# Window attention with sinks and a highway layer: K, Q and V loads issued at three points of a block, and the t bias in four pieces

## The chip, the cores and the metric

The kernel runs on one core of one Trainium2 chip. The metric is the device time of one execution in microseconds (us); the time before is the median of three runs. A second source is one execution recorded by the profiler. In it PE is the matmuls of TensorE, PEld its weight loads, DVE is VectorE, ACT is ScalarE, POOL is GpSimd, and SP issues DMAs.

## The reference

Attention with 4 sink keys and a window of 128, over 4 batches, 8 heads, 768 tokens and a head size of 64; then a highway layer on the 3072 tokens of 512 numbers.

```python
scores = q @ k.T / 8
keep = (key < 4) | ((row - key >= 0) & (row - key < 128))
a = softmax(where(keep, scores, -1e9))
x = (a @ v) as [3072, 512]
H = max(x @ w_h, 0)
T = 1 / (1 + exp(-(x @ w_t + b_t)))
out = T * H + (1 - T) * x
```

Inputs and output are 32-bit floats.

## The kernel before, in words

The tokens are cut into 24 blocks of 128, six for each batch. The key and value tiles lie half a block (64 tokens) off the query tiles, so that a query block meets its own shifted key tile in full and one half of each neighbour. For each block n the kernel does these steps, and a text called ORDER lists all steps of all blocks by hand as `step:block`. Each engine runs its own instructions in the order in which ORDER names them, so two neighbours on different engines may be exchanged there without a change in either engine's order.

- `S` (`pe_S`, L619): TensorE transposes the query and key tiles of a later block (L323; from block 8 on, S:n transposes q and k of block n+2) and makes the scores of block n (L376, L389). One query tile, that of block 9, has a transpose of its own, `Tq:9`.
- `xx` or `x0_`, `x1_`: ScalarE takes the exponential (L403, L398). `tt`, `tq`, `tk` copy the transposed tiles out of PSUM (L335, L328).
- `mm` or `m0_`, `m1_`: VectorE multiplies by the mask (L409).
- `sk`, `es`: scores and exponentials of the sink keys (L358, L365).
- `A` (`pe_A`, L445): values times weights. First `pe_AB` (L427) does the shifted halves as 16 matmuls of 64x64 (L434): their contraction rows are one half of the array's rows, their output partitions the other half. Then 8 full matmuls (L453) and 2 for the sinks (L459) follow.
- `xh` (L467, L472): VectorE normalises, the result is x in 16 bits. `X` transposes it (L486), `xT` or `xTV` copies it out.
- `Mh` (L514) and `Mt` (L502): four 512-column matmuls each with w_h and w_t. `u` is ScalarE's tanh (L507), `U` adds one (L526), `d` is max(h,0)-x (L520), `e` their product (L531), `o` the output (L536), which SP stores.

The bias b_t is added to the t product by a matmul with rows of ones. `bt16` holds half of b_t in rows 0 and 64 and zeros elsewhere. For blocks under 8, `pe_Mt` starts with one 128x128 matmul of 512 columns (L499). From block 9 on, `pe_A(n)` first calls `pe_bias(n-1)` (L439), which does the same for block n-1 with two matmuls of 64x64 and 512 columns (L442), one in rows and columns 0 to 63 of the array, one in 64 to 127. Two constant tiles serve this: `ones_row` (row 0 ones) and `ones2` (rows 0 and 64 ones), both made by VectorE in step `mc`, `bias_rows` (L262).

Loads of q, k and v are DMAs that GpSimd issues, one after the other in its queue, each turning 32 bits into 16. Those of the first nine blocks are written out ahead of ORDER (L210 to L238), except q8. The rest belong to step A:n, in this order:

```python
load_v(n + 4)      # from 9
load_q(n + 6)      # from 8
load_k(n + 6)      # from 9
```

From block 9 on q and k have three buffers each (`late_pool`), so that q12 takes the buffer of q9 and k12 that of k9; v has five slots. A load whose buffer is still in use waits in GpSimd's queue, and all behind it wait too. A load that begins a batch (k12, v12 and so on) is two DMAs of half the size. GpSimd also fills the sink keys and values of batches 1 to 3 (`fill_ks`, L347, and `sink_v`, L186) when `tk` or `tt` has copied the first key tile of the batch.

Of the kernel before, what the change touches and what calls it, by code (L numbers as in the profile page):

```python
# [20 lines left out]
def kernel(  # L21
# [18 lines left out]
    nc = tc.nc  # L40
# [46 lines left out]

    ctx.callback(close_s)
    HP = P // 2
    B0 = 9  # L90
    M0 = 9
    FIRST = 9
    NV = FIRST + 5
# [15 lines left out]
    def load_q(n):  # L109
        b, c = divmod(n, NSC)  # L110
        qsd = (sd_pool if n < FIRST else late_pool).tile([P, H, D], FP16, tag="qsd", name="qsd")
        nc.gpsimd.dma_start(out=qsd, in_=q[b, :, c * P:(c + 1) * P, :].transpose([1, 0, 2]))  # L112
        q_sd[n] = qsd

    def load_k(n):
        ksd = (sd_pool if n < FIRST else late_pool).tile([P, H, D], FP16, tag="ksd", name="ksd")
        for rows, b, s0 in chunk_parts(n):
            nr = rows.stop - rows.start
            nc.gpsimd.dma_start(out=ksd[rows], in_=k[b, :, s0:s0 + nr, :].transpose([1, 0, 2]))  # L119
        k_sd[n] = ksd  # L120
# [20 lines left out]
    bt32 = const.tile([P, DM], FP32, tag="bt32")  # L141
    bt16 = const.tile([P, DM], FP16, tag="bt16")
    ones_row = const.tile([P, P], FP16, tag="ones_row")
    ones2 = const.tile([P, P], FP16, tag="ones2")
    kf_first = const.tile([P, H, D], FP32, tag="kf0", name="kf0")
    ident32 = const.tile([P, P], FP32, tag="ident32")
    ident2 = const.tile([P, P], FP16, tag="ident2")
    ks_bd = [const.tile([P, KW], FP16, tag=f"ks{i}", name=f"ks{i}") for i in range(2)]
    vs_bd = [const.tile([P, H, 65], FP16, tag=f"vs{i}", name=f"vs{i}") for i in range(2)]
# [112 lines left out]
    def bias_rows(_):  # L262
        nc.vector.memset(bt16, 0.0)
        nc.vector.memset(ones_row, 0.0)
        nc.vector.memset(ones_row[0:1, :], 1.0)
        nc.vector.tensor_copy(out=ones2, in_=ones_row)
        nc.vector.memset(ones2[HP:HP + 1, :], 1.0)

    def bias_half(_):
        for r in (0, HP):  # L270
# [13 lines left out]
    def m_tile():  # L284
        return m_bank[int(next(m_next))]
# [141 lines left out]
    def pe_AB(n):  # L427
        av = av_tile(n)
        nxt = v_ring[vi(n + 1)]
        prv = v_ring[vi(n - 1 if n % NSC else n)]  # L430
        lo, hi = slice(0, HP), slice(HP, P)
        for j in range(H):
            for src, part, vt, h in ((lo, hi, nxt, j), (hi, lo, prv, (j + 4) % H)):
                nc.tensor.matmul(  # L434
                    av[part, h // 4, h % 4, 0:_AVN], lhsT=e_at(n, h)[src, P:EW],
                    rhs=vt[src, 65 * h:65 * h + _AVN], start=(h % 4 == 0), stop=False,
                    skip_group_check=True)

    def pe_bias(n):  # L439
        t_of[n] = m_tile()  # L440
        for rows in (slice(0, HP), slice(HP, P)):
            nc.tensor.matmul(t_of[n][rows, :], lhsT=ones2[rows, rows], rhs=bt16[rows, :],  # L442
                             start=True, stop=False, skip_group_check=True)

    def pe_A(n):  # L445
        if n >= B0:
            pe_bias(n - 1)
        pe_AB(n)
        av = av_of[n]
        vt = v_ring[vi(n)]  # L450
        b, c = divmod(n, NSC)
        for h in range(H):
            nc.tensor.matmul(  # L453
                av[:, h // 4, h % 4, 0:_AVN], lhsT=e_at(n, h)[:, 0:P],
                rhs=vt[:, 65 * h:65 * h + _AVN], start=False,
                stop=False, skip_group_check=True)
# [174 lines left out]
    def new_T(m, g):  # L631
        if g and m and m % NSC == 0 and m < NB:
            fill_ks(m // NSC, nc.gpsimd)
            sink_v(m // NSC, nc.gpsimd)

    def do_A(n):
        pe_A(n)
        if FIRST <= n + 4 <= NB:
            load_v(n + 4)
        if AHEAD <= n + 6 < NB:  # L640
            load_q(n + 6)
        if FIRST <= n + 6 <= NB:
            load_k(n + 6)

    def norm(n):
        dve_rec(n)
# [2 lines left out]
    def spare(t):  # L649
# [5 lines left out]
        "tqV": lambda n: copy_T(n, 0, nc.vector.tensor_copy),  # L655
        "tkV": lambda n: copy_T(n, 1, nc.vector.tensor_copy),
        "xx": act_SS, "tt": both_T, "mm": dve_masks,
        "S": pe_S, "x0_": lambda n: act_S(n, 0), "x1_": lambda n: act_S(n, 1),
        "m0_": lambda n: dve_mask(n, 0), "m1_": lambda n: dve_mask(n, 1),
        "sk": pe_sink, "es": act_sink, "A": do_A, "xh": norm,  # L660
        "X": pe_X, "xT": act_X, "xTV": lambda n: act_X(n, nc.vector.tensor_copy),
        "Mh": pe_Mh, "Mt": pe_Mt, "u": act_u, "U": dve_U, "d": dve_d, "e": dve_e, "o": dve_o,
# [12 lines left out]
    }  # L675
    ORDER = """
    mz0_:0 ma:0 na:0 Tq:0 na:1 Tk:0 tq:0 mz1_:0 tk:0 ma:1 wA:0 wA:0 Tk:1 mc:0 cv:0 tk:1 fa:0
    wA:0 wA:0 wA:0 S:0 cv:1 x0_:0 fb:0 x1_:0 wA:0 wA:0 wA:0 wA:0 Tq:3 m0_:0 fc:0 tq:3 wA:0 Tk:2
    tk:2 m1_:0 fd:0 wA:0 wA:0 wA:0 wA:0 Tq:1 A:0 tq:1 S:1 xh:0 sk:1 x0_:1 x1_:1 Tq:2 m0_:1 X:0
    sk:3 xTV:0 es:1 Tk:3 m1_:1 tq:2 tk:3 wA:1 A:1 es:3 S:2 xh:1 x0_:2 x1_:2 Tk:4 m0_:2 sk:2  # L680
    tkV:4 X:1 es:2 m1_:2 S:3 xT:1 A:2 x0_:3 Mh:1 x1_:3 xh:2 tq:4 d:1 X:2 tk:5 Mh:0 xTV:2 m0_:3
    Mh:2 d:0 m1_:3 S:4 d:2 Mt:0 x0_:4 x1_:4 m0_:4 A:3 u:0 m1_:4 Mt:1 tq:5 xh:3 tk:6 U:0 sk:4 u:1
    e:0 S:5 es:4 o:0 X:3 x0_:5 U:1 sk:5 xTV:3 e:1 A:4 x1_:5 m0_:5 o:1 tq:6 Mt:2 xh:4 tk:7 es:5
# [8 lines left out]
    d:11 S:14 xT:12 U:11 A:13 e:11 xx:14 o:11 Mh:12 xh:13 tt:14 Mt:12 mm:14 X:13 d:12 u:12 S:15  # L692
# [4 lines left out]
    A:18 xx:19 U:16 e:16 sk:19 xh:18 Mt:17 es:19 mm:19 tt:19 Mh:17 o:16 u:17 X:18 S:20 d:17  # L697
    xT:18 U:17 A:19 xx:20 e:17 o:17 Mh:18 xh:19 tt:20 Mt:18 mm:20 X:19 u:18 S:21 xTV:19 d:18
    A:20 xx:21 U:18 e:18 sk:21 o:18 Mt:19 es:21 xh:20 tt:21 Mh:19 mm:21 u:19 X:20 S:22 d:19
    xT:20 U:19 A:21 xx:22 e:19 o:19 Mh:20 xh:21 tk:24 Mt:20 mm:22 X:21 u:20 S:23 xTV:21 d:20  # L700
    A:22 xx:23 U:20 e:20 sk:23 xh:22 Mt:21 es:23 mm:23 X:22 u:21 Mh:21 xT:22 o:20 A:23 d:21 U:21
# [45 lines left out]
```

## Time and profile before

| What | Value |
|---|---|
| median of three runs | 120.45 us (120.37 to 120.69) |
| the profiled execution, its own time | 134.59 us |
| its span, first to last instruction | 132.5 us |
| granted TensorE clock in it, mean | 0.760 of full speed |
| GpSimd's load instruction (q, k, v) | 0.91, 0.86, 0.85 us each |
| from issue to landing, median (q, k, v) | 5.7, 5.7, 5.4 us |
| t bias before A, L442 | 30 matmuls, 0.42 us each, busy 6.4 us in all |
| shifted value matmuls, L434 | 384, busy 11.2 us in all |
| `u` plus one on VectorE, L526 | 23, 0.40 us in the mean, 0.28 to 1.13 |

The profiled execution is slower than the timed ones, so its durations are read with its own time beside them. A matmul's busy time contains its pipeline, so that matmuls overlap and a start says more than an end. A row of a timeline has the start, the length, the engine, the line of the kernel, the operation and its tiles (output<-inputs), and in brackets how long the engine was idle before it and what ended that.

### The profile page before, as it was taken

How to read it: one execution, taken by the hardware profiler on the slowest of the kernel's cores; microseconds unless marked ns; L12 is line 12 of the kernel's file. 1: busy time of each engine (PE TensorE's matmuls, PEld its weight loads, DVE VectorE, ACT ScalarE, POOL GpSimd, SP SyncE). 2: the span in 40 equal slices, each digit the busy share in tenths (PEclk: the TensorE clock that was granted, in tenths of full speed). 3: DMA queues.
4: the chain of work that ended last, by engine and by line, in shares of the span. 5: the costliest groups of instructions: out<-in, count | busy, mean ns of one | idle time of the engine just before them, and what ended most of it. 6: DMA issues, size and time to landing. Idle time of an engine off the chain costs nothing.

```text
span 132.5 us, 4975 instructions
## 1 busy us (share of the span) xinstructions
PE 122.8 (93%) x2119; PEld 69.7 (53%) x2119; DVE 106.5 (80%) x254; ACT 88.0 (66%) x123; POOL 72.2 (55%) x97
## 2 busy tenths in 40 slices
PE   5998879997999999999999999999999999999940
PEld 2444556444555464754666556647655664565520
DVE  6889745959897769968978797689979978977980
ACT  3356679196696668848977888768769868673120
POOL 6999878589940069926749466596591400000000
PEclk9977777777777777777777777777777777777775
DMA  3999999999999039999599999999999392202122
GB/s 90 217 158 147 161 181 195 155 138 123 185 194 153 2 90 190 190 196 137 56 178 158 153 161 140 171 97 96 180 187 131 103 127 84 79 5 79 54 105 79
DMA packets 79848, 17.64 MB, mean 133 GB/s; under 512 B 75602, under 2 KB 76882, under 8 KB 79828
## 3 DMA queue, kind: packets, MB, share of 16 engines
q0 software_dynamic: 71888, 9.97, 121.7%
q1 hardware_dynamic: 6884, 7.12, 17.7%
q10 hardware_dynamic: 1056, 0.26, 1.2%
q8 instruction: 16, 0.26, 0.8%
q14 instruction: 4, 0.03, 0.1%
HBM read 21.01 MB, written 6.29 MB: 206 GB/s over the span
## 4 chain that ended last, share of the span: by engine, by line
PE 81%; DVE 12%; ACT 2%; issue 2%; DVEq 0%
PE m L514 20%; PE m L502 19%; PE av L453 7%; PE av L434 6%; PE sps L323 5%; PE sps L376 4%; PE av L459 4%; PE sps L389 4%; PE m L358 4%; PE av L486 4%; PE m L499 2%; ACT e L398 1%; DVE u L526 1%; PE m L442 1%; DVE v L178 1%
## 5 line engine op out<-in xcount | busy, mean ns | idle before, releaser
L126 POOL DMA_DIRECT2D v<-in_v_dram x26 | 22.1, 853 | 18.4 <-PE av L434 14.0
L502 PE MATMUL m<-wt_sb,xT 128*128 128x512 f16 x92 | 30.4, 463 | 0.0
L514 PE MATMUL m<-wh_sb,xT 128*128 128x512 f16 x92 | 29.5, 458 | 0.0
L112 POOL DMA_DIRECT2D qsd<-in_q_dram x23 | 20.8, 908 | 11.9 <-PE sps L323 11.9
L403 ACT ACTIVATE e<-sps,ebias 128x1536 f16<-128x1536 f32 x15 | 23.1, 1541 | 4.4 <-PE sps L389 4.3
L409 DVE TENSOR_TENSOR e<-e,mask 128x768 f16<-128x768 f16 (+1 forms) x33 | 23.9, 732 | 2.5 <-ACT e L398 2.5
L507 ACT ACTIVATE u<-m 128x512 f16<-128x512 f32 x23 | 13.8, 598 | 13.7 <-PE m L502 13.7
L119 POOL DMA_DIRECT2D ksd<-in_k_dram x26 | 22.1, 856 | 0.5 <-DMA ksd<-in_k_dram 0.3
L398 ACT ACTIVATE e<-sps,ebias 128x768 f16<-128x768 f32 x18 | 15.2, 897 | 6.7 <-PE sps L389 6.5
L520 DVE SCALAR_TENSOR_TENSOR dd<-m,xh 128x512 f16<-128x512 f32 x23 | 15.8, 688 | 4.6 <-PE m L514 4.4
L472 DVE TENSOR_TENSOR xh<-av,rec 128x512 f16<-128x512 f32 x24 | 16.6, 691 | 0.8
L514 PEld LDWEIGHTS <-xT 128*128 128x128 f16 x92 | 10.0, 112 | 12.1 <-issue 10.8
L536 DVE SCALAR_TENSOR_TENSOR otok<-xh,ee 128x512 f32<-128x512 f16 x23 | 15.8, 689 | 0.6
L502 PEld LDWEIGHTS <-xT 128*128 128x128 f16 x92 | 9.9, 110 | 11.4 <-issue 10.8
L335 ACT COPY tt<-sps 128x1024 f16<-128x1024 f16 x13 | 13.0, 997 | 0.0
L434 PE MATMUL av<-v,e 64*64 64x66 f16 x384 | 11.2, 196 | 1.3 <-DVE xT L491 1.1
L491 ACT COPY xT<-av 128x512 f16<-128x512 f16 x15 | 8.7, 581 | 4.9 <-PE av L486 4.9
L526 DVE TENSOR_SCALAR u<-u 128x512 f16<-128x512 f16 x23 | 9.2, 400 | 2.9 <-ACT u L507 2.8
L434 PEld LDWEIGHTS <-e 64*64 64x64 f16 x384 | 9.5, 109 | 2.9 <-issue 2.3
L328 ACT COPY t<-sps 128x512 f16<-128x512 f16 x19 | 10.3, 589 | 1.1 <-PE sps L323 1.1
L453 PE MATMUL av<-v,e 128*128 128x66 f16 x192 | 10.7, 198 | 0.0
L486 PEld LDWEIGHTS <-xh 64*128 64x128 f16 x192 | 4.2, 95 | 11.6 <-DVE e L409 7.9
(94 smaller groups left out, 183.3 us busy)
## 6 DMA issues: line engine op xcount, KB each, us to landing
out_dram<-otok SPq DMA_DIRECT2D x23, 256.0 KB, 3.2
qsd<-in_q_dram POOLq DMA_DIRECT2D x23, 128.0 KB, 5.7
ksd<-in_k_dram POOLq DMA_DIRECT2D x19, 128.0 KB, 5.7
v<-in_v_dram POOLq DMA_DIRECT2D x19, 128.0 KB, 5.4
wh_sb<-in_moe_w_h_dram POOLq DMA_DIRECT2D x1, 512.0 KB, 7.5
wt_sb<-in_moe_w_t_dram POOLq DMA_DIRECT2D x1, 512.0 KB, 8.9
ksd<-in_k_dram POOLq DMA_DIRECT2D x7, 64.0 KB, 5.2
v<-in_v_dram POOLq DMA_DIRECT2D x7, 64.0 KB, 5.5
```

What stands on the lines that cost most here:

```text
L112: nc.gpsimd.dma_start(out=qsd, in_=q[b, :, c * P:(c + 1) * P, :].transpose([1, 0, 2]))
L119: nc.gpsimd.dma_start(out=ksd[rows], in_=k[b, :, s0:s0 + nr, :].transpose([1, 0, 2]))
L126: nc.gpsimd.dma_start(out=vt[rows, :, 0:D], in_=v[b, :, s0:s0 + nr, :].transpose([1, 0, 2]))
L398: nc.scalar.activation(out=e_tile(n)[:, g].rearrange("p a b c -> p a (b c)"), in_=s_tile(n, g)[:, :, 0:2 * EW], func=AF.Exp, bias=ebias, s ...
L403: nc.scalar.activation(out=e_tile(n).rearrange("p g a b c -> p (g a) (b c)"), in_=s_of[n][:, :, 0:2 * EW], func=AF.Exp, bias=ebias, scale= ...
L409: nc.vector.tensor_tensor(out=ev, in0=ev, in1=m.unsqueeze(1).to_broadcast([P, k, EW]), op=ALU.mult)
L434: nc.tensor.matmul(av[part, h // 4, h % 4, 0:_AVN], lhsT=e_at(n, h)[src, P:EW], rhs=vt[src, 65 * h:65 * h + _AVN], start=(h % 4 == 0), sto ...
L453: nc.tensor.matmul(av[:, h // 4, h % 4, 0:_AVN], lhsT=e_at(n, h)[:, 0:P], rhs=vt[:, 65 * h:65 * h + _AVN], start=False, stop=False, skip_g ...
L472: nc.vector.tensor_tensor(out=xh.rearrange("p (h d) -> p h d", d=D), in0=av_of.pop(n)[:, :, 0:D], in1=rec_of.pop(n).unsqueeze(2).to_broadc ...
L502: nc.tensor.matmul(t_of[n], lhsT=xT[:, kc, :], rhs=wt_sb[:, kc, :], start=False, stop=(kc == NOC - 1), skip_group_check=True)
L514: nc.tensor.matmul(hps, lhsT=xT[:, kc, :], rhs=wh_sb[:, kc, :], start=(kc == 0), stop=(kc == NOC - 1))
L520: nc.vector.scalar_tensor_tensor(out=dd, in0=h_of.pop(n), scalar=0.0, in1=xh_of[n], op0=ALU.max, op1=ALU.subtract)
```

## The change

It has four parts.

1. `pe_bias` and `ones2` go. `pe_AB(n)` now takes the bias of block n-1 itself: after each second pair of shifted matmuls (j = 0, 2, 4, 6) it does a pair of bias matmuls of 64x64 and 128 columns, so eight of 128 columns instead of two of 512. `ones_row` becomes block-wise: row 0 has ones in columns 0 to 63, row 64 in columns 64 to 127.
2. The load of q moves to step S: S:n loads q(n+5).
3. The load of k moves to step d: the d steps, in the order in which they stand, load k9, k10 and so on, from the third on. Before each, GpSimd copies one element of that step's result dd into a tile `turn`, so that the load stands behind a wait for VectorE. The load of v stays with A.
4. In ORDER, `fb:0` goes ahead of `x0_:0` and `cv:1` behind it (fb and cv are both on VectorE). Four other pairs of neighbours are exchanged, each on two different engines: xh:4 and tk:7, d:12 and u:12, d:17 and xT:18, xh:22 and Mt:21.

```diff
-    B0 = 9
+    T_BESIDE = {9: 8, 10: 9, 11: 10, 12: 11, 13: 12, 14: 13, 15: 14, 16: 15, 17: 16, 18: 17, 19: 18, 20: 19, 21: 20, 22: 21, 23: 22}
+    LATE = 9
...
-    ones2 = const.tile([P, P], FP16, tag="ones2")
+    turn = const.tile([1, 1], FP16, tag="turn")
...
-        nc.vector.memset(ones_row[0:1, :], 1.0)
-        nc.vector.tensor_copy(out=ones2, in_=ones_row)
-        nc.vector.memset(ones2[HP:HP + 1, :], 1.0)
+        nc.vector.memset(ones_row[0:1, 0:HP], 1.0)
+        nc.vector.memset(ones_row[HP:HP + 1, HP:P], 1.0)
...
+        m = T_BESIDE.get(n)
+        if m is not None:
+            t_of[m] = m_tile()
...
         for j in range(H):
             for src, part, vt, h in ((lo, hi, nxt, j), (hi, lo, prv, (j + 4) % H)):
                 nc.tensor.matmul(
                     av[part, h // 4, h % 4, 0:_AVN], lhsT=e_at(n, h)[src, P:EW],
                     rhs=vt[src, 65 * h:65 * h + _AVN], start=(h % 4 == 0), stop=False,
                     skip_group_check=True)
-
-    def pe_bias(n):
-        t_of[n] = m_tile()
-        for rows in (slice(0, HP), slice(HP, P)):
-            nc.tensor.matmul(t_of[n][rows, :], lhsT=ones2[rows, rows], rhs=bt16[rows, :],
-                             start=True, stop=False, skip_group_check=True)
+            if m is not None and n >= LATE and j % 2 == 0:
+                cols = slice(D * j, D * j + 2 * D)
+                for part in (lo, hi):
+                    nc.tensor.matmul(
+                        t_of[m][part, cols], lhsT=ones_row[part, part], rhs=bt16[part, cols],
+                        start=(j == 0), stop=False, skip_group_check=True)
...
-        if n >= B0:
-            pe_bias(n - 1)
...
+    def do_S(n):
+        pe_S(n)
+        if AHEAD <= n + 5 < NB:
+            load_q(n + 5)
+
+    k_next = iter(range(AHEAD - 1, NB + 1))
+
+    def do_d(n):
+        dve_d(n)
+        m = next(k_next, None)
+        if m is not None and m >= FIRST:
+            nc.gpsimd.tensor_copy(out=turn, in_=dd_of[n][0:1, 0:1])
+            load_k(m)
...
-        if AHEAD <= n + 6 < NB:
-            load_q(n + 6)
-        if FIRST <= n + 6 <= NB:
-            load_k(n + 6)
...
-    wA:0 wA:0 wA:0 S:0 cv:1 x0_:0 fb:0 x1_:0 wA:0 wA:0 wA:0 wA:0 Tq:3 m0_:0 fc:0 tq:3 wA:0 Tk:2
+    wA:0 wA:0 wA:0 S:0 fb:0 x0_:0 cv:1 x1_:0 wA:0 wA:0 wA:0 wA:0 Tq:3 m0_:0 fc:0 tq:3 wA:0 Tk:2
```

More of the change, by code (lines that the diff above doesn't have):

```diff
@@ L431, in pe_AB @@
         lo, hi = slice(0, HP), slice(HP, P)
+        m = T_BESIDE.get(n)
+        if m is not None:
+            t_of[m] = m_tile()
+            if n < LATE:
+                for part in (lo, hi):
+                    nc.tensor.matmul(
+                        t_of[m][part, :], lhsT=ones_row[part, part], rhs=bt16[part, :],
+                        start=True, stop=False, skip_group_check=True)
         for j in range(H):
@@ L437, in pe_AB @@
                     skip_group_check=True)
-    def pe_bias(n):
-        t_of[n] = m_tile()
-        for rows in (slice(0, HP), slice(HP, P)):
-            nc.tensor.matmul(t_of[n][rows, :], lhsT=ones2[rows, rows], rhs=bt16[rows, :],
-                             start=True, stop=False, skip_group_check=True)
+            if m is not None and n >= LATE and j % 2 == 0:
+                cols = slice(D * j, D * j + 2 * D)
+                for part in (lo, hi):
+                    nc.tensor.matmul(
+                        t_of[m][part, cols], lhsT=ones_row[part, part], rhs=bt16[part, cols],
+                        start=(j == 0), stop=False, skip_group_check=True)
     def pe_A(n):
-        if n >= B0:
-            pe_bias(n - 1)
         pe_AB(n)
@@ L657 @@
         "xx": act_SS, "tt": both_T, "mm": dve_masks,
-        "S": pe_S, "x0_": lambda n: act_S(n, 0), "x1_": lambda n: act_S(n, 1),
+        "S": do_S, "x0_": lambda n: act_S(n, 0), "x1_": lambda n: act_S(n, 1),
         "m0_": lambda n: dve_mask(n, 0), "m1_": lambda n: dve_mask(n, 1),
@@ L661 @@
         "X": pe_X, "xT": act_X, "xTV": lambda n: act_X(n, nc.vector.tensor_copy),
-        "Mh": pe_Mh, "Mt": pe_Mt, "u": act_u, "U": dve_U, "d": dve_d, "e": dve_e, "o": dve_o,
+        "Mh": pe_Mh, "Mt": pe_Mt, "u": act_u, "U": dve_U, "d": do_d, "e": dve_e, "o": dve_o,
         "mz0_": first_mask, "mz1_": second_mask, "id": identities, "ma": clear_ks,
@@ L682 @@
     Mh:2 d:0 m1_:3 S:4 d:2 Mt:0 x0_:4 x1_:4 m0_:4 A:3 u:0 m1_:4 Mt:1 tq:5 xh:3 tk:6 U:0 sk:4 u:1
-    e:0 S:5 es:4 o:0 X:3 x0_:5 U:1 sk:5 xTV:3 e:1 A:4 x1_:5 m0_:5 o:1 tq:6 Mt:2 xh:4 tk:7 es:5
+    e:0 S:5 es:4 o:0 X:3 x0_:5 U:1 sk:5 xTV:3 e:1 A:4 x1_:5 m0_:5 o:1 tq:6 Mt:2 tk:7 xh:4 es:5
     u:2 m1_:5 X:4 S:6 xT:4 U:2 e:2 A:5 x0_:6 o:2 Mh:3 x1_:6 xh:5 tq:7 Mh:4 m0_:6 tk:8 m1_:6 X:5
@@ L691 @@
     S:13 xT:11 U:10 A:12 e:10 xx:13 o:10 sk:13 xh:12 Mt:11 es:13 tt:13 mm:13 Mh:11 u:11 X:12
-    d:11 S:14 xT:12 U:11 A:13 e:11 xx:14 o:11 Mh:12 xh:13 tt:14 Mt:12 mm:14 X:13 d:12 u:12 S:15
+    d:11 S:14 xT:12 U:11 A:13 e:11 xx:14 o:11 Mh:12 xh:13 tt:14 Mt:12 mm:14 X:13 u:12 d:12 S:15
     xT:13 U:12 e:12 xx:15 A:14 o:12 sk:15 xh:14 Mt:13 tt:15 mm:15 es:15 X:14 S:16 u:13 xTV:14
@@ L696 @@
     xT:16 U:15 A:17 xx:18 e:15 o:15 Mh:16 xh:17 tt:18 Mt:16 mm:18 X:17 u:16 S:19 xTV:17 d:16
[L697 to L701, printed above, removed]
+    A:18 xx:19 U:16 e:16 sk:19 xh:18 Mt:17 es:19 mm:19 tt:19 Mh:17 o:16 u:17 X:18 S:20 xT:18
+    d:17 U:17 A:19 xx:20 e:17 o:17 Mh:18 xh:19 tt:20 Mt:18 mm:20 X:19 u:18 S:21 xTV:19 d:18 A:20
+    xx:21 U:18 e:18 sk:21 o:18 Mt:19 es:21 xh:20 tt:21 Mh:19 mm:21 u:19 X:20 S:22 d:19 xT:20
+    U:19 A:21 xx:22 e:19 o:19 Mh:20 xh:21 tk:24 Mt:20 mm:22 X:21 u:20 S:23 xTV:21 d:20 A:22
+    xx:23 U:20 e:20 sk:23 Mt:21 xh:22 es:23 mm:23 X:22 u:21 Mh:21 xT:22 o:20 A:23 d:21 U:21
     Mt:22 xh:23 e:21 X:23 u:22 Mh:22 xTV:23 o:21 Ta:23 d:22 Ha:23 ua:23 U:22 e:22 Tb:23 da:23
```

## The prediction

> **What bounds the kernel now.** I read first the busy times and the slices of the page, then busy times by stretch, then the waits, then the timelines of a steady block, of GpSimd's queue and of the start.
>
> ```profile
> PE 122.8 (93%) x2119; PEld 69.7 (53%) x2119; DVE 106.5 (80%) x254; ACT 88.0 (66%) x123; POOL 72.2 (55%) x97
> ...
> PEclk9977777777777777777777777777777777777775
> ```
>
> ```profile
> 42.00:54.00 12.00, 12.00 (x177) 6.11 (x175) 9.62 (x21) 8.91 (x16) 6.54 (x9) 0.75 0.74 102
> ...
> 63.00:72.05 9.05, 9.05 (x192) 5.41 (x190) 7.82 (x16) 7.46 (x10) 6.50 (x8) 0.75 1.24 131
> ```
>
> From 42 us on TensorE has no idle time (stretch rows: length, then busy PE, PEld, DVE, ACT, POOL), and its granted clock was 0.75. So in this execution each stall of TensorE after 42 us moves the end in full. It is not the timed kernel: it took 134.59 us (span 132.5 and 2.1 around it), the median is 120.45. Without the first 14 us, which VectorE paces, timed runs need (120.45-2.1-14)/(132.5-14) = **0.88** of the profiled time. The same 106.5 us of VectorE work are 90% of a timed span of 118.35 us. Intervals that TensorE paces shrink to 0.88; GpSimd issues and DMA latencies, I assume, do not. That is the heart of what follows.
>
> ```profile
> POOL v L126 <- PE av L434: 14.0, 7, 4.5
> POOL qsd L112 <- PE sps L323: 11.9, 2, 9.4
> ```
>
> ```profile
> 36.24 0.91 POOL L119 DMA_DIRECT2D ksd<-in_k_dram  x1
> 37.10 0.92 POOL L126 DMA_DIRECT2D v<-in_v_dram  x1
> 47.45 0.89 POOL L112 DMA_DIRECT2D qsd<-in_q_dram  x1 [9.43 <-PE sps L323]
> 48.33 1.39 POOL L119 DMA_DIRECT2D ksd<-in_k_dram  x2
> 49.68 0.92 POOL L126 DMA_DIRECT2D v<-in_v_dram  x1
> ```
>
> ```profile
> 46.86 0.29 PE L323 MATMUL sps<-ident,qsd 64*128 64x64 f16 x8
> ...
> 53.32 0.32 PE L323 MATMUL sps<-ident,ksd 64*128 64x64 f16 x8
> ```
>
> These are GpSimd's waits, two stretches of its queue (start, length, instruction, idle time before it) and two transposes. GpSimd waits for buffers, and after the first 17 us no engine that computes waits for a load. One wait is long: at 37.10+0.92 it reaches the load of q12, whose buffer is q9's, and stands 9.43 us until step Tq:9 has transposed q9 (46.86 to 47.15). What stands behind q12 in that queue is the question of this case.
>
> [...] here q12 took 3.6 us with nothing ahead of it, the loads 5.4 to 5.7 in the median. I use the trace. [...] the tensor_scalar on u (L526) lasts 282 ns at best and up to 1127, with GpSimd busy in all seven cases over 400. [...]
>
> **Part 1, the bias.**
>
> ```profile
> 72.07 0.43 PE L442 MATMUL m<-bt,ones 64*64 64x512 f16 x2
> 72.09 0.45 PE L434 MATMUL av<-v,e 64*64 64x66 f16 x16
> 72.47 0.43 PE L453 MATMUL av<-v,e 128*128 128x66 f16 x8
> ```
>
> The two 512-column matmuls already run beside the shifted ones: those start 0.02 us later and the full-array matmuls 0.38 us after them. Removing the lead gives 15 blocks x 0.02 = 0.3 us at most. The sixteen start over 0.45-0.19 = 0.26 us, 34 ns a pair, so a piece comes each 68 ns; its 128 columns take 278/4 = 69 ns (L502, four in 1.11 us on the chain). It just fits. Six more matmuls and weight loads a block go in slots that start a few ns apart. Bounds: -0.3 us, and +15 x 0.28 = +4.2 us if no piece overlapped. I take -0.1. If cover failed, each piece would cost its 69 ns.
>
> **Part 2, the start.**
>
> ```profile
> 7.72 0.17 DVE L265 MEMSET ones_row<- 1x128 f16 x1
> 7.92 0.29 DVE L266 COPY ones<-ones_row 128x128 f16<-128x128 f16 x1
> 8.29 0.17 DVE L267 MEMSET ones<- 1x128 f16 x1
> ```
>
> The copy goes (7.92 to 8.29, 0.37 us with its gap) and two memsets halve: 0.45 us of VectorE, which is on the chain here. The chain comes to A:0, where TensorE starts the bulk at 12.95; Tq:1 before it waits for its DMA and ends at 12.65. So 0.30 us at most. Nothing is later than that at once, but Mt:0 (26.5) needs wt, landed at 24.4, and in a faster run that eats some. I take -0.3, bounds 0 and -0.45. The swap of fb and cv:1 has one answer: both are VectorE steps whose inputs are long there, the sum is unchanged: 0. The other swapped steps are neighbours on different engines; no engine's own order changes: 0.
>
> **Part 3, the loads.** A step that moves takes its DMAs past others in GpSimd's queue. Written out around q12 from the order of steps:
>
> ```
> before: v9 q11 k11 | v10 q12 k12 | v11 q13 k13
> after:  q10 q11 v9 | turn k10 | q12 | turn k11 | v10 | turn k12 | q13 v11
> ```
>
> Before, k11 stands ahead of q12 (issued at 36.24, 17 us early). After, it stands behind, and so do v10 and k12. TensorE transposes k11 in S:9, at 53.32. The k12 halves at 48.33 and 49.00 took that place before: they took 5.2 us each, landing at 53.55 and 54.21, the same bytes behind the same q12 among the same stores. With one copy more (a memset here takes 0.1 us, L347's copies 0.2 to 0.34; I take 0.1 for one element) k11 lands at about 54.0: 6.85 us after Tq:9. TensorE needs it 53.32-47.15 = 6.17 us after, or 6.17 x 0.88 = 5.43 in a timed run. **Stall: 0.7 us profiled, 1.4 timed.** Low end: 47.45+0.89+0.1+3.6 = 52.0, no stall; high end, at full clock (6.17 x 0.75 = 4.6): 2.2. Behind TensorE at S:9 stand A:8, Mh:7, Mt:7, X:8; the exponential of block 9 and its mask wait. In a timed run VectorE has 2.1 us (d, u, e, o of block 6: 0.69+0.28+0.42+0.69) to do meanwhile, so I let 0.7 of the stall pass to the end: **+1.0**.
>
> k12 moves into the place of q13, which landed at 57.22, 10.1 us after Tq:9; S:10 needs it 58.42-47.15 = 11.3 us after, 9.9 timed plus the stall before it: nothing more.
>
> The second place is k20. Before, its load stands ahead of the fills of the sinks of batch 3; after, it stands behind them and behind d:14. The fills take 1.72 us from the end of tt:10 (61.65 to 63.37). tt:16 ends at 87.69, so k20 starts at 87.69+1.72+0.2 and, with 4.4 us of latency (between 3.6 and 5.1), lands at 94.0. TensorE wants it at 94.38, or 6.69 x 0.88 = 5.9 us after tt:16 in a timed run, against 6.3. Stall 0 profiled, 0.4 timed (0 to 1.1), of which 0.7 passes: **+0.3**.
>
> Elsewhere the moves cost nothing: k(n+7) is issued at the end of d(n), 0.3 us for wait and copy, 4.4 to 5 us of landing, against 7.8 us or more until its transpose in S(n+5) (d:9 ends at 67.70, k16 is needed at 76.00), 6.9 timed. If that cover goes, one block's transposes wait. q and v loads keep 6 us. The new waits hold GpSimd alone; behind them stand at most q(n+8), v(n+6) and the fills. The reads by `turn` hold dd's buffer until d(n+3), over 10 us later: 0. SP's queue keeps its stores.
>
> Gain of the spread: u (L526) exceeds 283 ns by 2.6 us in all. The one at 36.50 (+0.48) has an idle GpSimd after; those at 63.0, 71.84 and 99.5 (+0.26, +0.13, +0.30) may run before k is issued, since u follows d at once and the copy comes first. Bounds 0 and -1.2; VectorE is close to the bound only in timed runs, so -0.3.
>
> **Sum.** Profiled: 134.59 -0.3 -0.1 +0.7 +0 = 134.9. Timed: 120.45 -0.3 -0.1 -0.3 +1.0 +0.3 = **121.1**.
>
> **Rivals.** (A) k11 and k20 come in time: the loads after Tq:9 land in 3.6 to 4.4 us, as a lone one does. Then 120.45-0.7 = 119.8, faster. For it: q12's own 3.6. Against: the two k12 halves. It decides where k11 lands within 5.4 us of Tq:9. (B) The stall is filled by backlog and the gains are off the path: 120.4. For it, 80% of VectorE and 66% of ScalarE; against, TensorE's full rows. (C) The pieces do not fit between the pairs; at half their time 15 x 0.14 = 2.1 us: 122.5, with 0.07 a block as the point from which it outweighs the gains. Against it, 0.02 us between bias and shifted matmuls now. That the move of loads does nothing is B too.
>
> **Numbers.** The forecast (120.5 to 122.2) has 0.55, A 0.25, B 0.12, C 0.08. A change within 0.3%, 0.36 us, cannot be told from none here. Faster: A without its edge, 0.23. Same: B and the edges of A and of the forecast, 0.17. Slower: 0.60. The range reaches from A's middle, less some start gain, to C's: 119.5 to 122.7.
>
> **What would show it.** k11 issued after 48 us, landing near 54, and TensorE or its weight load waiting for ksd at S:9: right. No wait on ksd there: step 3 is wrong, A or B. A wait on ksd near S:18: the second place. L453 starting more than 0.45 us after the first shifted matmul: C. A:0 not some 0.3 us earlier: step 2 wrong. u below 300 ns from block 9 on: the spread gains. A timed clock unlike 0.88 of the profile's pace would shift the stalls by its ratio.

## The result and the profile after

The changed kernel takes **127.48 us** (median of four runs, 126.28 to 128.40) against 120.41 us for the kernel before in the same comparison: ratio 1.0566, interval 1.0470 to 1.0661. It is slower, as forecast, but by 7.1 us where 0.7 was forecast, and outside the range. The run at 128.40 us, like some runs of every kernel here, was in a slower state of the chip; the ratios, and the times of the experiments below, are of the other runs alone.

The profiled execution of the changed kernel took 127.46 us, with a span of 125.7 us, so it is like the timed runs. The one shown of before is not: it ran at a granted clock of 0.76. A second profile of the unchanged kernel, at 0.993 with a span of 118.5 us (run e1 below), is therefore what the changed kernel is held against.

Busy times and the granted clock on the page of the changed kernel:

```profile
PE 108.5 (86%) x2209; PEld 66.3 (53%) x2209; DVE 104.4 (83%) x253; ACT 87.7 (70%) x123; POOL 77.4 (62%) x113
...
PEclk9999999999999999779999999999999999999996
...
q8 instruction: 17, 0.28, 0.9%
```

No engine has much more work (in e1 TensorE's matmuls are busy for 106.0 us, of a span of 118.5), but TensorE is now without a matmul for 17.2 us of the span, where e1 has 12.5. Three things are to be kept in mind. Two slices in the middle have a granted clock of 7 tenths, those around them 9. There are 90 matmuls and 90 weight loads more, the pieces of the bias. And the queue that the page calls instruction had one transfer more than before (17 for 16; each is 16 KB).

Lines are now those of the changed kernel: L113 and L120 are the loads of q and k, L653 is the copy into `turn`, L323 the transpose of q and k, L442 the shifted value matmuls, L449 the bias pieces, L459 the full value matmuls, L526 d and L532 u. Its waits (total, times, longest):

```profile
POOL turn L653 <- DVE dd L526: 11.8, 7, 3.0
...
PEld L323 <- DMA ksd<-in_k_dram: 4.5, 3, 3.1
...
POOL qsd L113 <- DVE otok L542: 4.3, 1, 4.3
PE sps L323 <- DMA ksd<-in_k_dram: 3.9, 3, 3.0
PEld L442 <- issue: 3.4, 8, 1.6
...
PE av L442 <- issue: 1.4, 1, 1.4
```

The reader is to see two new kinds of idle time of TensorE. One is a wait for a load of k, 3.1 us at the longest. The other is "issue", with nothing in the profile to wait for: 1.6 us at the longest ahead of the shifted matmuls, where e1 has 0.6.

**The wait for k11.** GpSimd's queue after Tq:9 (which TensorE ends at 43.38 here), and TensorE at S:9:

```profile
43.68 0.87 POOL L113 DMA_DIRECT2D qsd<-in_q_dram  x1 [4.29 <-DVE otok L542]
44.55 0.40 POOL L653 COPY turn<-dd 1x1 f16<-1x1 f16 x1
44.89 0.87 POOL L120 DMA_DIRECT2D ksd<-in_k_dram  x1
```

```profile
48.36 0.28 PE L323 MATMUL sps<-ident,qsd 64*128 64x64 f16 x8
48.48 0.28 PE L376 MATMUL sps<-t,t 64*128 64x128 f16 x4
51.70 0.35 PE L323 MATMUL sps<-ident,ksd 64*128 64x64 f16 x8 [2.95 <-DMA ksd<-in_k_dram]
51.87 0.41 PE L376 MATMUL sps<-t,t 64*128 64x128 f16 x4
```

q12 goes out 0.30 us after Tq:9 has freed its buffer, the same interval as in e1 (43.74 to 44.04), where the bracket names TensorE. Here it names an output step of VectorE that ended 0.13 us after Tq:9; in e2, which has no such wait, the interval is 0.30 us too, and e4 below shows that the buffer decides. k11 stands behind q12 and the copy, and lands at 51.66. TensorE has transposed q11 by 48.64 and begins with k11 at 51.70: **3.06 us** (its matmuls are idle for the 2.95 in the bracket).

**What follows the wait.** Busy times by stretch (length; then PE, PEld, DVE, ACT, POOL; then the granted clock, DMA share and GB/s):

```profile
48.30:51.70 3.40, 0.45 (x20) 0.28 (x20) 2.44 (x6) 0.85 (x2) 3.40 (x6) 1.00 1.81 182
51.80:55.20 3.40, 3.40 (x64) 2.73 (x63) 1.07 (x3) 1.79 (x2) 2.12 (x3) 0.50 2.07 194
55.20:59.00 3.80, 3.80 (x93) 2.37 (x92) 2.99 (x6) 2.65 (x4) 1.75 (x3) 1.00 1.03 68
```

After the stall TensorE works at half clock for 3.41 us (51.79 to 55.21). The reciprocal of block 8 (the first part of its step xh) starts 3.16 us later than in e1, that of block 9 4.46 us later: 1.3 us more. This is the least that the half clock adds, for it begins ahead of the first of the two, at 54.10. The reciprocal of block 7 was 0.2 us ahead of e1's, so 4.7 us came in these two blocks, of which 3.1 are the wait; the other 1.6 are an estimate for the half clock. It seems not to come in every execution: one run took 126.28 us at a mean clock of 0.994, two took 127.46 and 127.50 at 0.978 and 0.975, and 3.41 us at half clock in a span of 125.7 take 0.014 off the mean. So the fastest run had probably none, and the 1.2 us between it and the other two fit that.

**The issue gaps.** TensorE at A:18, with the rest of the bias and shifted pairs behind:

```profile
95.00 0.22 PE L442 MATMUL av<-v,e 64*64 64x66 f16 x2 [0.19 <-DVE xT L497]
95.00 0.24 PE L449 MATMUL m<-bt,ones_row 64*64 64x128 f16 x2
95.02 0.23 PE L442 MATMUL av<-v,e 64*64 64x66 f16 x3
96.69 0.21 PE L442 MATMUL av<-v,e 64*64 64x66 f16 x1 [1.44 <-issue]
96.70 0.24 PE L449 MATMUL m<-bt,ones_row 64*64 64x128 f16 x2
```

In the middle of a run of independent matmuls no matmul starts for 1.63 us. Gaps of this kind are counted from here on from one start to the next, which is about 0.2 us more than the idle time in the bracket. With TensorE's records numbered in order from 0, those longer than half a microsecond come only at numbers that are 193 plus a multiple of 256; such a number is called a border below. After the first 20 us they are at 2753 (0.70 us), 3009 (0.61) and 3521 (1.63). At each of these the last 16 KB transfer of the instruction queue had ended 1.23 to 1.61 us before TensorE went on (for 3521 it ran from 94.19 to 95.09). The trace has 4462 records of TensorE and 17 such transfers, the first one of before 4281 and 16: one for 262 and 268 records, close to the 256 between borders. From these numbers I read the gaps as TensorE without instructions, because a transfer came late; that is my estimate, and no event of the profile shows it.

After block 9 the lag behind e1 is 4.5 us; it is 5.2 us at block 15, 5.7 at 16, 7.1 at 18 and 7.2 at the end, so what is not the one wait and its half clock comes in these gaps.

### The profile page after: what moved, and what is told of

It is laid out like the page before. It is cut to its first block, busy times and chain, and to the rows that moved or that the text cites. A ratio compares the mean times of both kernels' runs of the same rounds, so it can differ in the third digit from the quotient of the medians.

```text
span 125.7 us, 5195 instructions
## 1 busy us (share of the span) xinstructions
PE 108.5 (86%) x2209; PEld 66.3 (53%) x2209; DVE 104.4 (83%) x253; ACT 87.7 (70%) x123; POOL 77.4 (62%) x113
## 4 chain that ended last, share of the span: by engine, by line
PE 39%; DVE 26%; DMA 11%; issue 11%; POOL 5%; ACT 5%; DVEq 0%; POOLq 0%; ACTq 0%
PE m L520 8%; PE m L508 6%; DMA qsd<-in_q_dram 6%; DMA ksd<-in_k_dram 5%; DVE xh L478 5%; DVE otok L542 5%; PE av L459 4%; DVE e L409 4%; PE av L442 4%; DVE dd L526 3%; PE sps L323 3%; ACT e L398 3%; DVE u L532 3%; PE sps L389 3%; PE av L492 2%
## 5 line engine op out<-in xcount | busy, mean ns | idle before, releaser
L113 POOL DMA_DIRECT2D qsd<-in_q_dram x23 | 20.8, 908 | 4.8 <-DVE otok L542 4.3
L508 PE MATMUL m<-wt_sb,xT 128*128 128x512 f16 x92 | 23.6, 379 | 0.0
L120 POOL DMA_DIRECT2D ksd<-in_k_dram x26 | 21.9, 844 | 2.8 <-issue 1.7
L520 PE MATMUL m<-wh_sb,xT 128*128 128x512 f16 x92 | 23.6, 382 | 0.0
L526 DVE SCALAR_TENSOR_TENSOR dd<-m,xh 128x512 f16<-128x512 f32 x23 | 15.7, 684 | 0.2 <-PE m L520 0.2
L520 PEld LDWEIGHTS <-xT 128*128 128x128 f16 x92 | 8.8, 99 | 8.9 <-issue 1.0
L473 DVE RECIPROCAL rec<-av 128x8 f32<-128x8 f32 x24 | 4.9, 203 | 10.3 <-PE av L465 7.2
L442 PE MATMUL av<-v,e 64*64 64x66 f16 x384 | 11.2, 195 | 2.4 <-issue 1.4
L508 PEld LDWEIGHTS <-xT 128*128 128x128 f16 x92 | 8.8, 98 | 8.0
L442 PEld LDWEIGHTS <-e 64*64 64x64 f16 x384 | 9.8, 109 | 4.4 <-issue 3.4
L653 POOL COPY turn<-dd 1x1 f16<-1x1 f16 x16 | 4.5, 282 | 11.8 <-DVE dd L526 11.8
L459 PE MATMUL av<-v,e 128*128 128x66 f16 x192 | 10.8, 198 | 0.4 <-issue 0.4
L323 PE MATMUL sps<-ident,ksd 64*128 64x64 f16 x184 | 6.6, 191 | 4.4 <-DMA ksd<-in_k_dram 3.9
```

Source lines behind the costliest of these rows:

```text
L442: nc.tensor.matmul(av[part, h // 4, h % 4, 0:_AVN], lhsT=e_at(n, h)[src, P:EW], rhs=vt[src, 65 * h:65 * h + _AVN], start=(h % 4 == 0), sto ...
L508: nc.tensor.matmul(t_of[n], lhsT=xT[:, kc, :], rhs=wt_sb[:, kc, :], start=False, stop=(kc == NOC - 1), skip_group_check=True)
L520: nc.tensor.matmul(hps, lhsT=xT[:, kc, :], rhs=wh_sb[:, kc, :], start=(kc == 0), stop=(kc == NOC - 1))
L526: nc.vector.scalar_tensor_tensor(out=dd, in0=h_of.pop(n), scalar=0.0, in1=xh_of[n], op0=ALU.max, op1=ALU.subtract)
```

## The experiments

Each ratio is against the kernel before, with its 95% interval.

**e1: the kernel before, unchanged**, for a trace at the timed clock.

> The kernel before, unchanged, to get a trace at the clock of the timed runs. Every theory expects 120.4 us. The theory that most of the loss is the wait for k11 at S:9 (3 us) expects no wait of TensorE on ksd or qsd after 17 us here. The rival that a full-clock TensorE also runs short of instructions or loads in the old kernel expects such gaps here too, over 1 us each.

Measured: 120.73 us, ratio 1.0018 (0.9982 to 1.0053); span 118.5 us at clock 0.993. In it the bias, the shifted and the full matmuls of A:18 follow one another, beside a copy on VectorE:

```profile
88.77 0.42 DVE L491 COPY xT<-av 128x512 f16<-128x512 f16 x1
88.88 0.39 PE L442 MATMUL m<-bt,ones 64*64 64x512 f16 x2
89.24 0.45 PE L434 MATMUL av<-v,e 64*64 64x66 f16 x16
89.62 0.43 PE L453 MATMUL av<-v,e 128*128 128x66 f16 x8
```

At every border of 256 from 12 us on, the transfer of instructions had ended 1.5 us or more before; no gap follows. Note also that the shifted matmuls start 0.36 us after the bias here, where the profile at 0.76 had 0.02 at A:11. They wait for xT, which copies out of their PSUM buffer: it ends at 89.19, they start at 89.24. In 14 of the 15 blocks with this bias the shifted matmuls were released by xT, up to 0.46 us after the bias had started. So at the timed clock the bias ran in a wait that TensorE had anyway.

**e2: the changed kernel with the old loads.** The bias pieces and the start stay.

```diff
         pe_S(n)
-        if AHEAD <= n + 5 < NB:
-            load_q(n + 5)
...
         dve_d(n)
-        m = next(k_next, None)
-        if m is not None and m >= FIRST:
-            nc.gpsimd.tensor_copy(out=turn, in_=dd_of[n][0:1, 0:1])
-            load_k(m)
...
             load_v(n + 4)
+        if AHEAD <= n + 6 < NB:
+            load_q(n + 6)
+        if FIRST <= n + 6 <= NB:
+            load_k(n + 6)
```

> The changed kernel with all loads of q, k and v back in step A and without the copies into turn; the bias pieces, the shorter start and the order of steps stay. If the loads make the whole loss: 120.0 to 120.5 us (0.1 to 0.4 below before). If the bias pieces cost something of their own (0.07 us a block or more): 121.5 us or more. If both have a share: in between.

Measured: 122.54 us, ratio 1.0166 (1.0075 to 1.0257). So the pieces have a cost of their own, or the start has.

**e3: the changed kernel with the old bias** (two matmuls of 512 columns ahead of the shifted ones; the new loads stay).

```diff
-    LATE = 9
+    LATE = 99
```

> The changed kernel with the bias again as two matmuls of 512 columns ahead of the shifted ones; the loads stay at their three points. If the loads make the whole loss: 127.5 us as the changed kernel. If the pieces have a share, lower by that share; if they are all of it, 120.4 us.

Measured: 125.37 us, ratio 1.0425 (1.0368 to 1.0481). The wait for k11 is there (2.9 us), then 3.41 us of half clock. From the two: the loads are the larger cost, what e2 keeps a second one.

**e4: the changed kernel with one buffer more.** q9 takes its buffer from the pool of the early blocks, so that q12 has nothing to wait for at Tq:9.

```diff
-        qsd = (sd_pool if n < FIRST else late_pool).tile([P, H, D], FP16, tag="qsd", name="qsd")
+        qsd = (sd_pool if n <= FIRST else late_pool).tile([P, H, D], FP16, tag="qsd", name="qsd")
```

> The changed kernel, but q9 takes a buffer of the early pool, so that q12 finds a free one and does not wait for Tq:9; k11, v10 and k12 behind it come earlier. If the queue behind q12 is most of the loss: the wait of TensorE for k11 at S:9 (3.05 us in the trace) is gone and the time is 124.5 to 125 us; if it is half hidden, 126. If the loss comes from k loads tied to step d all over the kernel, or from the pieces: 127 to 127.5.

Measured: 122.04 us, ratio 1.0144 (1.0077 to 1.0211). GpSimd's queue in its trace:

```profile
39.68 0.89 POOL L113 DMA_DIRECT2D qsd<-in_q_dram  x1
40.55 0.53 POOL L653 COPY turn<-dd 1x1 f16<-1x1 f16 x1
41.02 0.88 POOL L120 DMA_DIRECT2D ksd<-in_k_dram  x1
```

q12 and k11 go out 4 us earlier, no wait for ksd is left in the steady blocks and no half clock. This takes 5.4 us off the changed kernel, more than was expected, since the half clock goes with the wait: the order q12, k11 does no harm where q12 doesn't wait. What remains, 1.4%, is e2's 1.7% within the intervals.

**e5: the kernel before with the bias in pieces, all ahead of the shifted matmuls**: the same instructions as in the change, not interleaved.

```diff
-        for rows in (slice(0, HP), slice(HP, P)):
-            nc.tensor.matmul(t_of[n][rows, :], lhsT=ones2[rows, rows], rhs=bt16[rows, :],
-                             start=True, stop=False, skip_group_check=True)
+        for j in range(0, H, 2):
+            cols = slice(D * j, D * j + 2 * D)
+            for rows in (slice(0, HP), slice(HP, P)):
+                nc.tensor.matmul(t_of[n][rows, cols], lhsT=ones2[rows, rows],
+                                 rhs=bt16[rows, cols],
+                                 start=(j == 0), stop=False, skip_group_check=True)
```

> The kernel before with its bias in four pieces of 128 columns as in the changed one, but all eight matmuls ahead of the shifted ones. TensorE gets as many instructions as in the changed kernel, 12 more a block, and no interleaving. Theory: the 1.9 us of the bias are TensorE running out of instructions (idle 0.4 to 1.1 us at every 256th instruction of its list, three times): 121.8 to 122.8 us, and such gaps in the trace at records 256 apart. Rival: the pieces disturb the shifted matmuls among which they stand: 120.5 to 121.2 us, no gaps.

Measured: 122.77 us, ratio 1.0143 (1.0101 to 1.0185). The cost of the pieces is there without the interleaving, and so are the gaps, at the same record numbers as in e2: 2753 (1.14 us; in e2 0.40), 3009 (0.79; 0.72) and 3521 (0.96; 1.08). The first of them:

```profile
71.81 0.32 PE L389 MATMUL sps<-tt 64*64 64x64 f16 x15
73.07 0.19 PE L389 MATMUL sps<-tt 64*64 64x64 f16 x1 [0.95 <-issue]
73.07 0.36 PE L444 MATMUL m<-bt,ones 64*64 64x128 f16 x6
```

It falls between the 15th and the 16th of sixteen like matmuls, ahead of the bias pieces, so no bias matmul makes it by its own execution. What the variants share is the count: 15 blocks times six matmuls and six weight loads are 180 instructions more.

**e6: e2 with 98 more instructions at the start**: seven of eight warm-up matmuls, which TensorE runs while it waits for the first loads, are cut in eight.

```diff
-        for _ in range(n):
-            nc.tensor.matmul(w, lhsT=warm[:, 0:P], rhs=warm, start=True, stop=True)
+        for i in range(n):
+            for c in range(0, DM, D if i < n - 1 else DM):
+                cols = slice(c, c + (D if i < n - 1 else DM))
+                nc.tensor.matmul(w[:, cols], lhsT=warm[:, 0:P], rhs=warm[:, cols],
+                                 start=True, stop=True)
```

> The kernel of the old loads and the new bias, with seven of the eight warm-up matmuls of 512 columns cut in eight of 64, so 98 instructions more on TensorE at the start and the same columns. All later borders of 256 instructions move by 98. If TensorE runs short of instructions at those borders: the gaps seen at records 2753, 3009 and 3521 are gone from those places and stand, if at all, where the new borders are; the time is 121 to 123 us. If the gaps belong to the work that stands there (scores of block 13, values of 14 and 17): same places, 122.7 us.

Measured: from 124.05 to 129.77 us in four runs, above the 121 to 123 that were expected and too far apart for an interval: as a time it is inconclusive. The places of the gaps in its trace (of a run of 126.19 us) are clear. They are again at 193 plus a multiple of 256 (1985: 1.95 us, 3009: 0.90, 3777: 1.45), but at other work than in e2, since each instruction of the main part now has a number 98 higher. The largest falls into the full value matmuls, and half clock follows (0.50 from 56.7 to 60.0; from 53.3 to 56.6 it was 1.00, with matmuls busy for 1.54 us of the 3.30):

```profile
54.17 0.37 PE L461 MATMUL av<-v,e 128*128 128x66 f16 x6
56.29 0.22 PE L461 MATMUL av<-v,e 128*128 128x66 f16 x2 [1.76 <-issue]
```

So the gaps go with the place in the instruction list and not with the operation.

**e7: only the start** (and the order of fb and cv): LATE = 99 as in e3, loads as in e2.

> The changed kernel with the old loads and the old bias: what is left is the shorter start on VectorE and the order of fb and cv. The prediction gave this 0.3 us: 120.4 us. The traces so far show 0.26 us at block 0 and 0.85 from block 4 on: 119.9 us. If a later wait takes it back: 120.7.

Measured: 120.30 us, ratio 0.9992 (0.9955 to 1.0029). Not to be told from before. With e7 as the base the parts add up: bias pieces 122.54-120.30 = 2.2 us, loads 125.37-120.30 = 5.1 us, together 7.3 for the 7.1 us of the whole. e2 has only three such runs, and its interval is 1.1 us to either side.

**e8: e3 with q loaded in A again** (k still at d, with the copy).

```diff
         pe_S(n)
-        if AHEAD <= n + 5 < NB:
-            load_q(n + 5)
...
             load_v(n + 4)
+        if AHEAD <= n + 6 < NB:
+            load_q(n + 6)
```

> The changed kernel with the old bias, and the q loads back in step A; the k loads stay behind step d with their copies. In GpSimd's queue q12 then stands behind k10, k11 and v10. If the place behind q12 makes the wait for k11: no wait on ksd at S:9, no slow clock there, 121 to 121.5 us (old bias with all new loads: 125.4); k20 may still come late at S:18 (1.4 us there). If k behind step d is late by itself: a wait of 2 us or more at S:9, 124 to 125 us.

Measured: 122.25 us, ratio 1.0108 (0.9984 to 1.0231), somewhat over the 121 to 121.5 expected. k11 now stands ahead of q12; S:9 does not wait. A wait of 1.6 us from start to start is left at S:18, for k20:

```profile
84.12 0.28 PE L376 MATMUL sps<-tt 64*128 64x128 f16 x4
85.70 0.29 PE L323 MATMUL sps<-ident,ksd 64*128 64x64 f16 x8 [1.30 <-DMA ksd<-in_k_dram]
```

**e9: e3 with TensorE kept busy through the wait**: 16 matmuls of zeros ahead of k11's transposes, into a part of the scores' tile that is overwritten afterwards. It tests whether the half clock comes from the idle time.

```diff
             if hosted(n, g) is not None:
+                if n == 9 and g == 1:
+                    for _ in range(16):
+                        nc.tensor.matmul(s_tile(n, 1)[:, 0, 0:2 * EW], lhsT=warm[:, 0:P],
+                                         rhs=warm[:, 0:2 * EW], start=True, stop=True)
```

> The kernel of the new loads and the old bias, with 16 matmuls of 384 columns on zeros put into step S of block 9 between the transposes of q11 and of k11; their results are overwritten. They take 2.6 us of the 2.9 us in which TensorE waits for k11. The wait was followed by 3.4 us of a granted clock of 0.5. If idleness of TensorE brings the slow clock: no 0.5 there, values of block 8 to values of block 9 in 4.1 to 4.4 us in place of 5.6, and 124.0 to 124.5 us in all (125.4 without). If the slow clock has another cause: it stays, 125.4.

Measured: 126.03 us, ratio 1.0507 (1.0409 to 1.0605). The total missed: no gain over e3. The place itself did what was expected. TensorE at S:9, and the stretch after it, which in e3 has a clock of 0.54:

```profile
48.43 2.77 PE L630 MATMUL sps<-warm 128*128 128x384 f16 x16
51.14 0.29 PE L323 MATMUL sps<-ident,ksd 64*128 64x64 f16 x8
```

```profile
51.00:54.60 3.60, 3.60 (x72) 2.40 (x71) 1.88 (x4) 2.69 (x3) 2.67 (x4) 1.00 2.16 201
```

The load is late again (it lands at 50.35, in e3 at 51.01), but TensorE keeps its full clock. The 16 matmuls outlast the wait by 0.8 us, which is a cost of the test itself. From the reciprocal of block 8 to that of block 9 it takes 4.47 us in place of 5.62. By block 12 e9 is 1.76 us ahead of e3. It gives that back: a gap of 1.57 us at record 2497 (70.5 to 72.1; its 32 more instructions shift what stands at each border) and a wait for k20 of 1.9 us. That the half clock at this place came from the idle time is shown by the clock after it, 1.00 where e3 has 0.54; that it can be avoided for free is not.

**e10: e2 without most late loads.** It tests what delays the instructions. From block 14 on q, k and v aren't loaded: a tile of zeros is transposed for q and k, and v keeps old values. Part of the computation is left out.

```diff
     def load_q(n):
+        if n >= 14:
+            q_sd[n] = stale
+            return
```

> The kernel of the old loads and the new bias, without the loads of q, k and v from block 14 on: it transposes a tile of zeros in their place and leaves v as it was. If the load traffic delays the fetches of TensorE's instructions (which end 1.4 us before it goes on at each gap): no gap over 0.3 us at the borders of 256 from 70 us on, 119.5 to 120.5 us. If the fetches come late by themselves, because 256 instructions are used up faster than one fetch takes: gaps as before, 122.5 us.

Measured: 120.11 us, ratio 1.0020 (0.9945 to 1.0096), with all pieces in place. The time alone doesn't show that their cost is gone, since the old bias without these loads was not run; the borders say more. The DMA engines from 70 to 92 us in 40 slices, first e2, then e10:

```profile
DMA  9899999999999999999995100999999999999999
```

```profile
DMA  0006501000920010000000000598100007400010
```

At the five borders from 2497 to 3521 the transfer of instructions starts in e10 within 0.6 us of TensorE's passing the border at four (68.94 us for 68.87, 73.72 for 73.67, 85.52 for 84.99) and 1.4 us after it at one, in e2 1.9 to 3.3 us after it (69.80 for 67.50, 74.87 for 72.24, 87.74 for 84.44). The gaps at 2753 and 3521 are gone, that at 3009 falls from 0.72 to 0.21 us. Where e10 still has its loads it has gaps as well, 0.61 us at 961 and 0.83 at 1985. Nor is the old bias free of them: after 20 us e1 has none, e7 one of 0.72 us, e11 one of 0.67. But with the pieces there are three after 70 us, 2.2 to 2.9 us in all, in each of the changed kernel, e2, e4 and e5. So in these traces the three gaps come where both meet: the pieces, 12 instructions more a block, and DMA engines that are busy for nine tenths or more in most slices (e2's row above).

**e11: e3 with k loaded in A again** (q at S, no copy).

```diff
         dve_d(n)
-        m = next(k_next, None)
-        if m is not None and m >= FIRST:
-            nc.gpsimd.tensor_copy(out=turn, in_=dd_of[n][0:1, 0:1])
-            load_k(m)
...
             load_v(n + 4)
+        if FIRST <= n + 6 <= NB:
+            load_k(n + 6)
```

> The changed kernel with the old bias and the k loads back in step A, without copies; the q loads stay in step S. k11 and v9 then stand ahead of q12 in GpSimd's queue; v10 and k12 behind it, as k12 did before. If it takes both moves to put k11 behind q12: no wait on ksd at S:9, and none at S:18, since k20 goes ahead of the fills: 120.2 to 120.8 us. If q loads at S have a cost of their own: 121.5 or more.

Measured: 120.34 us, ratio 1.0033 (0.9963 to 1.0104). The move of q alone costs nothing that can be measured, that of k alone (e8) some 1.9 us against e7, though e8's interval reaches down to no cost; both together 5.1. The wait for k11 needs both: only then does k11 stand behind q12.

**e12: e3 with e4's buffer.** With neither pieces nor a wait for Tq:9, nothing but k20's place should be left.

> The changed kernel with the old bias and q9 in a buffer of the early pool: all loads at their new places, but nothing waits for Tq:9. The wait at S:9 should be gone, the one for k20 at S:18 (1.4 us with the old bias) should stay: 121 to 121.8 us. If k20 is in time too, since GpSimd is ahead by then: 120.2.

Measured: 122.7 us, ratio 1.0234 (1.0117 to 1.0351), above the 121 to 121.8 expected and no faster than e4, though it has less in it. The trace is of the longest of its runs, 124.86 us. S:9 doesn't wait. TensorE waits for k20 at S:18, and in this trace that wait too is followed by half clock:

```profile
85.58 0.28 PE L376 MATMUL sps<-tt 64*128 64x128 f16 x4
87.53 0.29 PE L323 MATMUL sps<-ident,ksd 64*128 64x64 f16 x8 [1.66 <-DMA ksd<-in_k_dram]
```

```profile
84.60:88.00 3.40, 1.73 (x52) 0.84 (x54) 3.33 (x6) 1.63 (x3) 3.40 (x5) 1.00 1.34 213
88.10:91.40 3.30, 3.30 (x45) 1.90 (x34) 1.94 (x4) 2.44 (x2) 2.00 (x3) 0.50 2.01 150
```

Its reciprocals are 1.0 us behind e1's at block 16 and 3.8 behind at block 18. In the changed kernel itself k20 comes in time (it lands at 90.05 and is transposed at 90.39), and so it does in e4 (84.55, 85.08). In both it lands 3.4 to 3.6 us after its issue, in e3, e8, e9 and e12 4.6 to 4.7; and S:18 comes 3.6 us after the issue in both, 2.6 to 3.0 in the others. What shortens the one and lengthens the other was not isolated.

No kernel here beats the one before: e7, e10 and e11 are level with it.

## Why the prediction was right or wrong

The step that failed is the sum. Its largest term, the stall for k11, was put at +1.0 us and was about 4.5: the wait itself was twice as long, none of it was made up, and the half clock behind it was not in the sum at all. The second is the bias, put at -0.1, which cost about 2 us, by my reading in instructions that came late.

**Part 3, the loads: mechanism right, three terms too small and one missing.** k11 behind q12 makes TensorE wait at S:9 (e4, e8 and e11 each take away the order or the wait, and the stall goes), and k20 is the second place (e3, e8, e9, e12).

- *"6.85 us after Tq:9"*: k11 landed 8.28 us after it (51.66-43.38). Of the 1.43 us more, 1.2 are in the landing: 6.76 us from issue, where 5.56 was put from the two halves of k12 (54.0 less 48.44). The rest is the copy: it delays the next issue by 0.34 us (44.55 to 44.89), not by 0.1. "The same bytes behind the same q12 among the same stores" was an assumption on the state of the DMA engines, read from a slower execution, as was that DMA latencies stay. The kernel before itself has medians of 6.5, 6.5 and 6.0 us to landing for q, k and v at the timed clock (e1), where the slower execution had 5.7, 5.7 and 5.4. That the same traffic in less time makes each load longer is the likely reason, not a shown one. The same load of k11 took 6.5 us in e3 and 5.7 in e9, so it also varies.
- *When TensorE needs it* was right: 48.64-43.38 = 5.26 us after Tq:9, where 5.43 was worked out. The ratio of 0.88 was good for this interval, though the clock was 0.98 for 0.76. The wait is then 8.28-5.26 = 3.0 us, above the high end of 2.2, which varied only the clock and kept the landing.
- *"I let 0.7 of the stall pass to the end"*: all of it passed, and more. From block 7 to block 8 the reciprocals lose 3.4 us on e1, and no later block recovers it. TensorE's rows in the steady blocks were full before (busy for 12.00 us of 12.00 from 42 us on, in the first profile), so there is nothing in which a late block could be made up.
- *The term that was missing is the half clock*: +1.3 us between blocks 8 and 9, about 1.6 in all; e9, which avoids it, is 1.76 us ahead of e3 by block 12. In the changed kernel the rate was 0.50 for 3.413 us, after the wait of 3.1 us; in e6 and e12 the same rate came after 1.9 us from one start to the next.
- *The second place, k20, "+0.3"*: 1.5 us of wait in e3, 1.6 in e8, 1.9 in e12, where 0.4 (0 to 1.1) was given. In e3 k20 is issued 2.5 us after tt:16 (1.9 in the sum) and lands 4.6 us later (4.4). The changed kernel does not wait here.
- *"Elsewhere the moves cost nothing"*: not quite. k9 keeps TensorE 0.5 us at S:7 in the changed kernel; it shows in block 6, ahead of the stall.
- *The gain of the spread, "-0.3"*: not seen. u exceeds 283 ns by 2.5 us in all in the changed kernel and by 1.3 in e1, which has the old loads.

**Part 1, the bias: the fit was right, what the instructions cost was left out.** The pieces do fit between the pairs. At A:11 the full matmuls start 0.38 us after the first shifted one, as before, and the point that would have spoken for rival C (0.45) isn't reached:

```profile
65.91 0.22 PE L442 MATMUL av<-v,e 64*64 64x66 f16 x2
...
66.29 0.43 PE L459 MATMUL av<-v,e 128*128 128x66 f16 x8
```

"Six more matmuls and weight loads a block go in slots that start a few ns apart" took the instruction as free once its slot is. In the runs it was not: 180 more of them cost about 2 us (2.2 as e2 less e7, 1.7 as e5's 1.43%), close to C's 2.1, but by another mechanism: e5 has the cost without C's interleaving, and e10 has C's interleaving without the gaps at 2753 and 3521 and with 0.21 us at 3009. That the gaps keep their place in the list when other work stands there (e6) and go when the load traffic goes (e10) supports late instructions; the profile has no event that says so directly. Nor was there the small gain: the bias ahead of A had filled a wait for xT (e1), which the pieces can no longer fill.

**Part 2, the start: no gain that can be measured.** A:0's full matmuls start 0.07 us earlier than in e1 in the changed kernel, 0.17 in e7, against 0.30. VectorE is out of the way there: A:0's full matmuls follow 0.60 us after Tq:1 in both, 0.95 in e1. But Tq:1 waits for its load, and it starts between 12.46 and 12.94 us in the eleven traces with the new start, between 12.30 and 12.37 in the three with the old. So a load that comes later takes most of the gain; why it does is open. The reciprocal of block 4 is 0.7 to 1.2 us earlier than in e1 in most of the traces, but as much in e5, which has the old start, and 0.7 us later in e12, which has the new one; so this place varies from trace to trace. e7 as a whole is level with before.

**The range** left out 127.5 because each bound varied one term with the others kept: the landing and the share that passes were on the low side at once, and neither the half clock nor the cost of 180 more instructions was in it. Rivals A and B fell with the wait itself, C by its own criterion.

## What to carry to other kernels

When a load moves in a queue, ask first which instruction ahead of it can wait, and price its landing with the range that the trace shows under load (5.7 to 6.8 us for k11 here), not with one pair of transfers. The stall of TensorE of 3.1 us cost its length here and then an estimated 1.6 us at half clock (of 4.7 us of lag in two blocks); stalls of 1.9 us were followed by half clock in e6 and e12 and not in e9. And with TensorE full of short matmuls and the DMA engines full too, the count of its instructions was a cost: 180 of them, which fitted into free slots, cost about 2 us (2.2 as e2 less e7).

## What was unexpected in the hardware

- **TensorE's gaps keep step with transfers of 16 KB.** The changed kernel has 17 of them for 4462 records of TensorE, the one before 16 for 4281 (its first profile), and the gaps stand 256 records, or a multiple of that, apart. With the DMA engines full (nine tenths or more in most slices of e2), such a transfer began as late as 5.4 us after TensorE had passed the border before (e9, at 69.3) and took 0.9 to 1.8 us. At the gaps of over half a microsecond TensorE went on 1.2 to 1.8 us after the transfer's end. In e2 that made three gaps, of 0.4 to 1.1 us, at seven borders after 70 us.
- **The granted clock changed in steps of 3.413 us.** In the changed kernel's trace the full clock lasts 44.37 us, 13 times 3.413, then half clock 3.413, then full clock 68.27, 20 times; in the first profile of before the clock of 0.75 lasts 122.88 us, 36 times. Ahead of the half clock matmuls were busy for 0.45 us of 3.40 in the changed kernel, 0.16 of 2.80 in e3 (48.2 to 51.0), 1.54 of 3.30 in e6 and 1.73 of 3.40 in e12. Cut into pieces of 3.413 us from its first change of clock on, the changed kernel's trace has matmuls busy for 2.26 us or more in every other piece of full clock up to 120.06, and none of those is followed by half clock; the gap of 1.63 us lies in two of them, which meet at 96.16. The length of the idle time alone does not part the cases: the wait for k20 left TensorE's matmuls idle for 1.66 us in e12, and half clock follows; for 1.67 in e9, whose mean clock is 0.998, and for 1.30 in e8 (0.995), and none follows. What parts them was not tested.
- **A copy of a single element on GpSimd** takes 0.28 us in the mean (16 in the changed kernel), and the next DMA issue started 0.18 to 0.67 us after the copy did.
